# Strassen's seven products for the outputs of chunk pairs in a fused GateLoop and PReLU MLP kernel

## The chip, the cores and the metric

The kernel runs on one core of a Trainium2 chip. The metric is the device time of one execution in microseconds (us). Everything is float32.

## The reference

A gated linear attention (GateLoop) with complex gates over 768 steps, 4 batches, 8 heads of 48 dimensions, followed by an MLP of width 384, 2048, 384 over all 3072 tokens, with a PReLU whose slope is given per feature.

```python
mag = np.sqrt(a_re * a_re + a_im * a_im)
scale = np.minimum(mag, 0.999) / (mag + 1e-06)
a_re_n, a_im_n = (a_re * scale, a_im * scale)
for t in range(S):
    ar, ai = (a_re_n[:, :, t, :, None], a_im_n[:, :, t, :, None])
    new_re = ar * S_re - ai * S_im
    new_im = ar * S_im + ai * S_re
    kv = np.einsum('bhd,bhe->bhde', k[:, :, t], v[:, :, t])
    S_re, S_im = (new_re + kv, new_im)
    y[:, :, t] = np.einsum('bhd,bhde->bhe', q[:, :, t], S_re)
...
x = attn_out.transpose(0, 2, 1, 3).reshape(B * S, H * D)
h = x @ w_in
g = np.maximum(h, 0.0) + alpha * np.minimum(h, 0.0)
return g @ w_out
```

## The kernel before

The 3072 tokens are 24 chunks (units) of 128, six to a batch. Four kinds of work run side by side:

- **Gates**: nine calls of `gates`, each for one to three chunks, turn a_re and a_im into phases and products of decays with VectorE (DVE) and ScalarE (ACT), some 42 steps on a buffer of 6918 columns (`gate`, two of them), and store them in DRAM. Call g loads its inputs when call g - 2 is done.
- **Units**: `unit(u)` loads q, k, phases and decays, and goes through the chunk in levels 1, 2, 4, ... 32: DVE multiplies a 96x1024 tile in place (L634), ACT makes copies (L657, L673), TensorE (PE) forms small products (L593) that DVE or ACT mask (L617, L607). Then come transposes (L705), state sums (L717, L746, L749) and the output y of the chunk (L737, L761), which ACT copies (L775) and SyncE (SP) stores.
- **Weights**: pieces of w_in and w_out are loaded into `g_sb`, converted and put in place. This happens in the first fifth of the run.
- **MLP**: chunks are put together in groups, `sizes` = 1, 1, ten times 2, 1, 1. For a group m and each of 16 blocks f of 128 features, `features` runs three matmuls of 128x128 weights on 256 columns (128 for a single chunk) into `ps_h` (L809), of which two buffers exist; ACT takes Relu(-h) into a place of `g_sb` (L816), and DVE adds alpha - 1 times h to make the gate (L818). `outputs` then multiplies the gate of one chunk with 384 columns of w_out (L828) and sums over the 16 blocks in `ps_o`, of which there is one. At the end of a chunk ACT copies the sum (L838) into one of two rows of `top`, and SP stores it (L841). Two output matmuls follow each block of features.

`g_sb` has 36 places, in three rings, that the raw weights use first.

The order of all of this is written out. Each task is a generator that yields once before each instruction or block of them, and ORDER is a string with one letter per step; `run` walks through it. A to I are the calls of gates, J to M loads and pieces, N and O the weights, P to Z and a to m the 24 units, n the loads of the MLP's inputs, o the whole MLP. An engine runs its own instructions in this order, so an instruction that waits holds up those behind it on its engine. The rings (`R`) and times in the yields are what a planner reads; in the kernel shown here they do nothing.

Of the kernel before, what the change touches and what calls it, by code (L numbers as in the profile page):

```python
# [9 lines left out]
F32 = mybir.dt.float32  # L10
# [5 lines left out]
ALU = mybir.AluOpType  # L16
# [12 lines left out]


ORDER = (
    "ABAMBMAAAABBAAAAABAAAAAAABMAAAMNNAANBBBBBAAAKKJJJMAAAMJANAAJAAAAAAAABBOBAAONNOOBBBBBOBBBBNNOMOONBPPP"
    "LJOCKJLLCPCCCNONONPCPPPBBLLLKMMMLLKKBBJBOCPCPNNPBCCPBCBBBBBPPPPNCNBNPNNCPJJLLLLLJLLMJPCBNNPPPNBNBBBP"
    "OPPPPOCOOCPCPPOPPPPPPPMCCNOOOCOOPPDJJJMJJJDCCNNNQDPDODNPPPPDPPQNQCOPQQQQNQCPPMJJMQCOQOQNODOQQDQOJCLL"
    "LMLLLLLQDQNOOCNOORORRRnCLLLLLLLMQDRQRQRQQQQQCRRQQQQDJJKJJJMKoQoQQQoQQQLLLLLLLDONCNRNCCRNOQQOOCQCCQCC"
    "RQRCROCRQNoooooQoDQRQQDoCLooLQooQCLLLLLLRODDDRRRRRoDOoRooooooNRRRRoooRRoNDDDRoooRoRRoRoRRNRSoRSNoDRO"
    "oMJJSoooNooooooRRNSoNNoRRJJRRSSSNooooooooooSSSooooSoSSooODSSoooooSSoOoNooooJJSSnooSoSOSSLJLLLLoooRRL"
    "LLoSDSSTToJLJLLLLLLJEJToSSoSooSOSoTSToOoooTDDDDoOTooooooSSSSSSTTSSSoSToooJJKLLJLLLLoooooTSSSSSTooTTD"
    "ooooToELJJLLooooDoToooooooTDDooooooooTDTTooJLLLJoToooToooUooooooLLUoooDTTTTTooooooooooooooooooooToDD"
    "ooTooDEToooooELTJJJnTooEoTTTDTTToTDDTTTDDooooVUTTEoooooTTTLLFJoEUooUUUVUVLLLooJJoJLLLLJoooUooUoooooo"  # L40
    "ooUooooooUUUooooUUUoooooVoVoUUoooUUoVUUUEooUVEUVoUooUooUoooUoVVEEoEVKJLLLLLUUUUUUUFLLLLLJKKUUUUEVUUU"
    "UVooooooEEooooVVooVoVEEooooVoEoKVoooooooooLLLLLLLLLLVVoEVVoVEoWVoonJJEVVVVooVEEVWVooooooVVVVVVVWoEEo"
    "JLLLLEJLLLEEooooEoWVVVWVWoWEWVEVooVVLLVVoooooWWooooJooEWFooooooooooWWFFLEWEJJJKJLLLJJLLooooooWWWXooo"
    "ooWWWWoXoooooWWWWWFWooWEEFEXEEEoFoooooWWoXooWWWWWWXXoJELLLJLooXWXXXLGLJLoooWWoooXWLLLooXWWXooLXXWWXW"
    "WXoooooooLXXXXXXXXXoooooLLoooooXoXWLGJJoXXooXXXXXoYXoGXYYXooooonJLLJJLKKKLJYoXooYYYYFXXFFYoXXoooYFoo"
    "ooooooYXXFoFoKXJoYYoooGYoYoYFYXFoooooooooFGLLLJLLLLJJJJLLLoooooYYYYYooZoooooZYFFYoooooJLoooYYoFoooYY"
    "ooZGooFFFoooYooZYZZZZoooooooJFFFZYYYYYZFLLLLZLLLFYYYYYYYYYYYoooooooooaYFFFaLLLJoJLJoLLJLLKoooooooKKJ"
    "JJFZZZoooooooZZFZooooooGooZZZZZZZooZZoZooZFFFoaGGooZZooGoaZZZZZoZFZFoFFZFnLLLLLooooooooaZZZZZZZZaGGa"
    "aaZbLFLooooooaooooooaobboooHHJLooaaooooaoooooooabaaooooLJJJLLLLLJoJoooooaaaaaaaaoooaoaooaGGHGaaHoooo"
    "ooooooGbGboGGoooooooaaaaaaaabaaaaaoGboobLLJbboooGbLaaJJHHoooooLLLLLJLLJJLoLoooobcoooooobbGoobbbcbooo"  # L50
    "ooccooooobooHooooobccbbbbbbccooHbbcbooooooooocboobLLLboocGGJnJccbobbbLGGGocbbbdcccdbooooobboLLLLLLLL"
    "LLGGGGGbbbbbobLLLLooccGcoooooocJJJcoHooooococccoGococooooccooooooHoccccccGGGGGcccccccoLLJJJJKLddoGoo"
    "HoGLLLoddoddHdccoccdoooooooooooodeooddodoHdHHdoooooodeoooJJLLLLLLLJJLLJJoooooooodddHHdeoooddoHdoHHed"
    "ddoooeeeedoooIIooddooododdddHddHnddHdddoddooHeeooooddJoooooooIeeeeeoHHeooooooofoeLLdLooooeoeeeoeeeee"
    "ooooJJHJLLLLLoLLLLLLLJJJeoeoofooffoeooJoffofofffooeooooofHHHooeoeIeeeeeeHeeeeeeIgIeIoooooooffooooffo"
    "oooogHffHooHoooooofffoffffHoooeLeLLLLJJLLLLLLLLLLJJJnfJgffooooooooooofoooHgffoggffooofgIJoIHHHHHHogg"
    "gooooofffgffffggffofofgoIggfgoooooIoooooooogghhIIoooooooIogfLLLfhhoooooooIoKLLLJJhJJJJJLLLLLLLLooooh"
    "ooooIIoggoooogohhhhoghggoogoooogoioooggoogggggohggggIIIIooooooggIoggoIooooigLLLgLLLLJJLJhhhJLKoooooo"
    "ooLhhhJJoIJohooooooooooooooohhoooLLLLLihoooohihhhhoohooooiiohhooIIInIohooooooohhhhhhLiihhhhhhhhhhhoo"
    "ooooooiooIIIiioohJJLLLLLLLJJLLLLLLJoooooooIooiiooooooooooiooooiiooooooIiooooooiiIIiiiioiiIooooooojjj"  # L60
    "iooooooIooiooooooijoooijjJJjkooiLikIiooooiiiijjjjoooooiIIiiooooijLLLLLIijiiLoojjjioiLiLijLooooLoLLoo"
    "oojjjoojjjoooojjjooojjooooooojooJLjLLJoojjjjjjjjjJJJJjjjjookjjjjkooooooLookkkkkkooookooooooookkkoook"
    "noooLLLLLJJJLLJLLJJLLLLooooooLllooookkooooooooookkkkkkoooolooookkoookookooookkkoooooookkkkkkkkolllll"
    "lloooooooooooooooooollkkkLlklllJLLLLLLLLLLLoLJoooooooLooookkkkknooooolllooololoooooooooooolllllllJLJ"
    "oooooolooooollloooooooooooooooooollllooooooooolooooooooooooooooooooooooooommmoooooomommmLLLLoooooooo"
    "mmmoooLooooooooooooooooooomolllllllloooommooLlLLlmoooooooooooomnLLLLLmmoooooooooooooooooommmoooooooo"
    "oooommmmmmmooooooooomoooooooooooooooLoooooooooooooooooooooomoooooomooooomoommmmoommmmmmmoooooommmnoo"
    "oooooooooooooooooooooooooooooooooooooooooooooooooooooooooooooooooooooooooooooooooooooooooooooooooooo"
    "ooooooooooooooooooooooooooooooo")


class Ring:
# [25 lines left out]
def kernel(  # L98
# [99 lines left out]
    def step(*args, **kwargs):  # L198
# [3 lines left out]

    R = {name: Ring(n) for name, n in dict(
        KQ=3, PP=1, T=2, V=1, WQ=2, W=1, St=3, xT=2, raw0=1, raw1=1, raw2=1, g0=0, g1=0, g2=0, ot=2, top=2,
        lv=2, misc=1, y=1, h=2, o=1).items()}
    for name in (1, 4, 16, 32):
        R[name] = Ring(2 if name == 1 else 1)


    scr_of = {}  # L210
    carry = consts.tile([P, NK], F32, tag="carry")
    bias_tiny = next(column)
# [16 lines left out]
    def gates(g, b, c0, c1):  # L229
# [4 lines left out]
        TT = nc.vector.tensor_tensor  # L234
        STT = nc.vector.scalar_tensor_tensor

        flat = work.tile([P, 6 * NK * GT + 2 * NK], F32, tag="gate", name="gate", bufs=2)
        x, c, d, e = [flat[:, i * N:(i + 1) * N] for i in range(4)]
        dec = flat[:, 2 * N:4 * N].rearrange("p (m s) -> p m s", s=TL)
        wide = [flat[:, 4 * N + i * NK * (n + 1):4 * N + (i + 1) * NK * (n + 1)] for i in range(2)]  # L240
# [5 lines left out]

        for z, src in ((rows3(x), a_re), (y, a_im)):
            rows = src[b].rearrange("n i d s -> (n i d) s").rearrange("(t p) s -> p t s", p=P)
            t = yield DMA(N / 2, ("gates", g - 2))
            if last:  # L250
                nc.gpsimd.memset(z[:, :, n - 1:n], 0.0)
            nc.sync.dma_start(z[:, :, 0:n - last], rows[:, :, c0 * P + 1:c1 * P + 1 - last])
            if z is y:
                ty = t
            else:
                tx = t
# [108 lines left out]
    tops = [consts.tile([P, 2 * DM], F32, tag=f"top{i}", name=f"top{i}") for i in range(2)]  # L365
    slots = [0, 1]
    raws = {}

    g_sb = consts.tile([P, 3, 6 * MT], F32, tag="g_sb")

    def region(i):
        return (i + 2) % 3
# [181 lines left out]
    nc.gpsimd.memset(nothing, 0.0)  # L554
    nothing = nothing.bitcast(BF16)

    sizes = [1, 1] + [MC] * ((NU - 4) // MC) + [1, 1]
    group_of = [(g, c) for g, n in enumerate(sizes) for c in range(n)]

    def unit(u):  # L560
# [240 lines left out]
    def features(m, f):  # L801
# [8 lines left out]
                             start=(kk == 0), stop=(kk == NK - 1))  # L810
        if f == NF - 1:
            R["xT"].put(e)
        i, ring, half = place(m, f)
        r = yield ACT(n, e, takes=() if half == 1 else (ring,), first=True)
        gt = g_sb.rearrange("p r (f s) -> p (r f) s", f=12)[:, i:i + sizes[m]].rearrange("p f s -> p (f s)")
        nc.scalar.activation(gt, p, AF.Relu, scale=-1.0)  # L816
        r = yield DVE(n + 45, r, first=True)
        nc.vector.scalar_tensor_tensor(out=gt, in0=gt, scalar=al_1[:, f:f + 1], in1=p,  # L818
                                       op0=ALU.mult, op1=ALU.add)
        R["h"].put(r)  # L820
        return gt, r

    def outputs(m, c, f, gt, r):

        e = yield PE(0.645, r, ("w_out", f), takes=() if f else (R["o"],))
        if f == 0:
            sums[0] = ps.tile([P, DM], F32, tag="o", name="ps_o")
        nc.tensor.matmul(sums[0], lhsT=gt[:, c * P:(c + 1) * P], rhs=w_out_sb[:, f],  # L828
                         start=(f == 0), stop=(f == NF - 1))
        if c == sizes[m] - 1:  # L830
            _, ring, half = place(m, f)
            if half != 0:
                ring.put(e)
        if f == NF - 1:
            row = (sum(sizes[:m]) + c) * P
            t = yield ACT(DM, e, takes=(R["ot"],))
            ot = tops[0].rearrange("p (c e) -> p c e", c=2)[:, (row // P) % 2]
            nc.scalar.activation(ot, sums[0], AF.Copy, scale=4.0 if words else 1.0)  # L838
            R["o"].put(t)
            t = yield DMA(197, t)  # L840
            nc.sync.dma_start(out[row:row + P], ot)  # L841
            R["ot"].put(t)

    sums = {}

    def all_mlp():


        made, jobs = {}, [(m, c, f) for m, n in enumerate(sizes) for c in range(n) for f in range(NF)]
        for m in range(len(sizes)):  # L850
            for f in range(NF):
                new = yield from features(m, f)
                for _ in range(2):
                    if jobs[0][0::2] not in made:
                        break
                    j = jobs.pop(0)
                    yield from outputs(*j, *made[j[0::2]])
                    if j[2] == NF - 1:
                        break
                made[m, f] = new  # L860
        for j in jobs:
            yield from outputs(*j, *made[j[0::2]])


    for h in LEVELS[:4]:
# [55 lines left out]
```

## Time and profile before

| | |
|---|---|
| median of three runs | 814.46 us (810.97 to 818.67) |
| profiled execution | 812.23 us |
| its span, first to last instruction | 810.5 us |
| mean granted clock of PE | 0.975 |
| PE busy | 697.3 us (86%) |
| DVE busy | 564.4 us (70%) |
| ACT busy | 457.0 us (56%) |
| DMA moved | 130.58 MB, mean 161 GB/s |

Busy time is the union of an engine's instructions. Matmul records overlap, so the time that one takes from the next is read from their starts. A line such as L809 is a line of the kernel before; the rows that name a line give the operation, the tiles written and read, the size, the count, then busy time in us and mean ns, then the engine's idle time just before and what ended it. Every float32 matmul of the program leaves two matmul records and two weight loads (PEld).

The features of the MLP's groups start on PE at 104.8, 164.4, 195.4, 240.7, 303.3, 361.0, 419.3, 478.6, 537.6, 592.5, 648.7, 700.8, 746.5 and 784.0 us.

### The profile page before, as it was taken

The page shows a single profiled execution, that of the slowest core. Times are in us where ns is not written, and L with a number is a line of the kernel's source. Part 1 is how long each engine was busy: PE and PEld are TensorE (multiplying, and loading weights), DVE is VectorE, ACT ScalarE, POOL GpSimd, SP SyncE. Part 2 cuts the span into 40 slices and gives each one's busy share as a digit, 9 for nine tenths or more (in the row PEclk, how much of TensorE's full clock was granted, in tenths as well). Part 3 has the DMA queues.
Part 4 walks back from the last instruction along what each step waited for, and adds up shares of the span by engine and source line. Part 5 has one row for each costly group of instructions (what it writes and reads, how often), then busy time and mean ns, then how long its engine had stood idle before and what let it go on. Part 6 is the DMA issues. An engine that isn't in the chain of part 4 may idle for free.

```text
span 810.5 us, 26318 instructions
## 1 busy us (share of the span) xinstructions
PE 697.3 (86%) x11488; PEld 522.7 (64%) x11488; DVE 564.4 (70%) x799; ACT 457.0 (56%) x897; POOL 11.9 (1%) x49
## 2 busy tenths in 40 slices
PE   0014167899999999999999999999999999999998
PEld 0013155678777667767777777777777777777776
DVE  6889998878898778786787977887466455154122
ACT  8999894775667447746574558454644333222221
POOL 4000000000000000000000000000000000000000
PEclk9998578999999999999999999999999999999999
DMA  8989998687778596677548765784653743301010
GB/s 231 292 271 249 247 235 225 152 231 200 183 203 212 161 241 141 171 196 176 148 116 228 189 164 139 200 175 114 175 121 101 166 99 100 75 12 36 28 31 10
DMA packets 177578, 130.58 MB, mean 161 GB/s; under 512 B 66296, under 2 KB 168824, under 8 KB 177016
## 3 DMA queue, kind: packets, MB, share of 16 engines
q1 hardware_dynamic: 177464, 128.91, 60.9%
q8 instruction: 90, 1.47, 0.8%
q14 instruction: 24, 0.20, 0.1%
HBM read 100.52 MB, written 35.42 MB: 168 GB/s over the span
## 4 chain that ended last, share of the span: by engine, by line
PE 67%; ACT 14%; DVE 8%; DMA 6%; issue 3%; SPq 2%; POOL 0%; ACTq 0%; DVEq 0%; POOLq 0%
PE ps_o L828 26%; PE ps_h L809 26%; PE ps_lv L593 5%; PE ps_y L737 3%; DVE KQ L634 3%; PE ps_y L761 2%; PE ps_kv L717 2%; DMA T<-decs 2%; PE ps_kt L705 2%; ACT WQ L657 1%; DMA VL<-vsc 1%; DMA PP<-phs 1%; DMA g_sb<-in_w_in_dram 1%; ACT top L426 1%; DVE gate L304 1%
## 5 line engine op out<-in xcount | busy, mean ns | idle before, releaser
L809 PE MATMUL ps_h<-xT,w_in_sb 128*128 128x256 f32 (+1 forms) x1344 | 301.2, 355 | 0.0
L828 PE MATMUL ps_o<-w_out_sb,g_sb 128*128 128x384 f32 x768 | 296.2, 497 | 4.2 <-DVE g_sb L818 3.5
L809 PEld LDWEIGHTS ps_h<-xT,w_in_sb 128*128 128x128 f32 x1344 | 233.1, 192 | 71.3 <-DVE g_sb L818 1.8
L818 DVE SCALAR_TENSOR_TENSOR g_sb<-g_sb,al,ps_h 128x256 f32<-128x256 f32 (+1 forms) x224 | 97.6, 438 | 160.5 <-ACT g_sb L816 160.0
L816 ACT ACTIVATE g_sb<-ps_h 128x256 f32<-128x256 f32 (+1 forms) x224 | 78.4, 352 | 190.9 <-PE ps_h L809 189.9
L634 DVE TENSOR_TENSOR KQ<-KQ,T 96x1024 f32<-96x1024 f32 x120 | 145.9, 1217 | 48.4 <-PE ps_lv L593 38.0
L828 PEld LDWEIGHTS ps_o<-w_out_sb,g_sb 128*128 128x128 f32 x768 | 135.5, 190 | 53.9 <-DVE g_sb L818 6.2
L593 PE MATMUL ps_lv<-WQ 96*32 96x32 f32 x2304 | 34.4, 202 | 56.0 <-DVE WQ L576 38.8
L593 PEld LDWEIGHTS ps_lv<-WQ 96*32 96x32 f32 x2304 | 26.3, 115 | 78.1 <-DVE WQ L576 32.9
L657 ACT COPY WQ<-KQ 96x1024 f32<-96x1024 f32 x48 | 49.9, 1040 | 25.5 <-DVE KQ L634 25.5
L775 ACT COPY T<-ps_y 48x256 f32<-48x256 f32 x96 | 31.6, 364 | 39.7 <-PE ps_y L761 38.9
L737 PE MATMUL ps_y<-A,VL 64*48 64x64 f32 x2304 | 43.8, 225 | 7.3 <-issue 3.7
L607 ACT ACTIVATE A<-ps_lv,columns 128x64 f32<-128x64 f32 x144 | 37.5, 337 | 20.1 <-PE ps_lv L593 20.0
L737 PEld LDWEIGHTS ps_y<-A,VL 64*48 64x48 f32 x2304 | 40.2, 126 | 10.8 <-issue 6.5
L673 ACT COPY W<-KQ 96x512 f32<-96x512 f32 x48 | 30.6, 638 | 28.3 <-DVE KQ L634 27.2
L593 PE MATMUL ps_lv<-KQ,W 96*32 96x32 f32 x1536 | 24.2, 203 | 25.3 <-ACT W L673 24.9
L593 PEld LDWEIGHTS ps_lv<-KQ,W 96*32 96x32 f32 x1536 | 19.4, 114 | 27.8 <-ACT W L673 26.2
L705 PE MATMUL ps_kt<-ident,KQ 96*128 96x96 f32 x192 | 26.0, 260 | 13.0 <-ACT T L708 6.7
L705 PEld LDWEIGHTS ps_kt<-ident,KQ 96*128 96x128 f32 x192 | 20.9, 147 | 23.8 <-ACT T L708 9.1
L707 ACT COPY T<-ps_kt 128x384 f32<-128x384 f32 x48 | 23.1, 480 | 18.8 <-PE ps_kt L705 18.6
L717 PEld LDWEIGHTS ps_kv<-V,T 64*64 64x64 f32 x1408 | 26.6, 142 | 9.5 <-ACT T L708 5.0
L617 DVE TENSOR_TENSOR A<-ps_lv,mask 128x512 f32<-128x512 f32 x48 | 32.7, 681 | 0.0
(85 smaller groups left out, 696.5 us busy)
## 6 DMA issues: line engine op xcount, KB each, us to landing
T<-decs SPq DMA_DIRECT2D x48, 384.0 KB
PP<-phs SPq DMA_DIRECT2D x24, 387.0 KB
KQ<-in_q_dram SPq DMA_DIRECT2D x48, 192.0 KB
phs<-gate SPq DMA_DIRECT2D x14, 577.5 KB
decs<-gate SPq DMA_DIRECT2D x7, 1152.0 KB
KQ<-in_k_dram SPq DMA_DIRECT2D x40, 192.0 KB
vsc<-in_v_dram SPq DMA_DIRECT2D x24, 288.0 KB
VL<-vsc SPq DMA_DIRECT2D x48, 144.0 KB
```

The costliest lines, as they stand in the source:

```text
L593: nc.tensor.matmul(t[64 * i + j:64 * i + j + HC // 2, p], lhsT=keys(n, g), rhs=queries(n, g), start=True, stop=True)
L607: nc.scalar.activation(a[:, :, cols], t[:, :, at:at + name], AF.Copy, scale=s)
L617: nc.vector.tensor_tensor(out=a.rearrange("p l n (g t) -> p l n g t", g=2), in0=t.unsqueeze(3).to_broadcast(whole), in1=pairs[first].rearr ...
L634: nc.vector.tensor_tensor(out=x, in0=x if x0 is None else x0, in1=m, op=ALU.mult)
L657: nc.scalar.copy(z.rearrange("p i n t -> p i (n t)").rearrange("p i (m h) -> p m i h", h=h), bass.AP(tensor=KQ.tensor, offset=KQ.offset + ...
L705: nc.tensor.transpose(t[:, p], KQ[:, 1, 4 * i + p], ident[:D2, :D2])
L717: nc.tensor.matmul(kv[s][j:j + HC, n], lhsT=T[rows, n, j:j + HC], rhs=V[rows, n // 2, (n % 2) * D:(n % 2 + 1) * D], start=True, stop=True)
L737: nc.tensor.matmul(o, lhsT=Vp[h][64 * i:64 * i + 64, s, e_ * D:(e_ + 1) * D], rhs=a, start=False, stop=False)
L809: nc.tensor.matmul(p, lhsT=w_in_sb[:, f // 2, kk, f % 2 * P:(f % 2 + 1) * P], rhs=x_of[m][:, kk], start=(kk == 0), stop=(kk == NK - 1))
L816: nc.scalar.activation(gt, p, AF.Relu, scale=-1.0)
L818: nc.vector.scalar_tensor_tensor(out=gt, in0=gt, scalar=al_1[:, f:f + 1], in1=p, op0=ALU.mult, op1=ALU.add)
L828: nc.tensor.matmul(sums[0], lhsT=gt[:, c * P:(c + 1) * P], rhs=w_out_sb[:, f], start=(f == 0), stop=(f == NF - 1))
```

## The change

The last two chunks become a pair, so that `sizes` is 1, 1 and eleven times 2. Groups 0 to 2 are computed as before. From group 3 on, the outputs of a pair are a product of two by two blocks: rows are the two chunks, the inner dimension is halved (features 0 to 1023 and 1024 to 2047), and the columns are halved (192 each). Strassen's scheme in Winograd's form takes seven products of blocks, P1, P2, T2, T3, T4, T1 and P3, of eight matmuls on 192 columns each, where eight products would be 32 matmuls on 384 columns. The blocks of gates are kept by quarters (four blocks f of one chunk, 512 columns) in `spread`, 13 quarters in all. S1 to S4, sums of gate blocks, are eight DVE operations per pair on whole quarters; sums of blocks of w_out are made once (`twist`, `twist_last`). The products are read out of the two halves of one PSUM tile, P1 by ACT, the others by DVE, which adds what was summed before and writes parts of the result.

A half of a product follows each block of features; P1 and S3 come in the second half of the pair's own features, the others in those of the next pair.

`spread`, the sums of w_out, `g_sb` and the gates of call 1 share one SBUF area. Of `gate` there is one buffer left, and from call 3 on call g loads when call g - 1 is done. ORDER is new.

```diff
     R = {name: Ring(n) for name, n in dict(
...
-        lv=2, misc=1, y=1, h=2, o=1).items()}
+        lv=2, misc=1, y=1, h=2, o=1, sums=0, fourth=0).items()}
...
+    GATE = 6 * NK * GT + 2 * NK
+    QUARTER, HALF = NF // 4, DM // 2
+    shared = consts.tile([P, 18 * MT + GATE], F32, tag="shared")
+    g_sb = shared[:, 0:18 * MT].rearrange("p (r e) -> p r e", r=3)
+    spread = shared[:, 0:13 * QUARTER * P].rearrange("p (h f s) -> p h f s", f=QUARTER, s=P)
...
-        flat = work.tile([P, 6 * NK * GT + 2 * NK], F32, tag="gate", name="gate", bufs=2)
+        if g in (1,):
+            flat = shared[:, 18 * MT:18 * MT + GATE]
+        else:
+            flat = work.tile([P, GATE], F32, tag="gate", name="gate", bufs=1)
...
-            t = yield DMA(N / 2, ("gates", g - 2))
+            t = yield DMA(N / 2, ("gates", g - 2 if g < 3 else g - 1))
...
-    sizes = [1, 1] + [MC] * ((NU - 4) // MC) + [1, 1]
+    sizes = [1, 1] + [MC] * ((NU - 2) // MC)
+    FIRST = 3
...
+            r = yield ACT(n, e, takes=() if f % QUARTER else (R["fourth"],) * 2, first=True)
+            if f % QUARTER == 0:
+                two = sorted(free[0:2])
+                free[0:2] = []
+                quarter[m, f // QUARTER] = two
+            a, b_ = quarter[m, f // QUARTER]
+            gt = spread[:, a:b_ + 1:b_ - a, f % QUARTER]
+            p = p.rearrange("p (c s) -> p c s", c=2)
...
+    def twist():
+        for name, dst, x, y, op in (("T3", T3, B22, B12, ALU.subtract), ("T2", T2, T3, B11, ALU.add),
+                                    ("T4", T4, B21, T2, ALU.subtract)):
+            for i in range(2):
+                some = slice(i * F2 // 2, (i + 1) * F2 // 2)
+                t = yield DVE(F2 * HALF // 2, ("gates", 1), ("w_out", NF - 1))
+                nc.vector.tensor_tensor(out=dst[:, some], in0=x[:, some], in1=y[:, some], op=op)
...
+    def seven(m, made):
...
+        def product(blocks, w, name, after, let_go=True):
+            if not bank:
+                bank.append(ps.tile([P, 2, HALF], F32, tag="o", name="ps_o"))
+                bank.append(0)
+            z = bank[0][:, bank[1] % 2]
+            bank[1] += 1
+            for i in range(F2):
+                h = blocks[i // QUARTER]
+                e = yield PE(0.325, after[i // QUARTER], known.get(name), takes=() if i else (R["sums"],))
+                nc.tensor.matmul(z, lhsT=spread[:, h, i % QUARTER], rhs=w[:, i], start=i == 0, stop=i == F2 - 1)
...
+        z, e = yield from product(A11, B11, "P1", [F(0), F(1)], let_go=False)
+        for i in range(2):
+            t = yield DVE(QUARTER * P, F(i), takes=(R["fourth"],))
+            S3[i] = free.pop(0)
+            TT(out=whole(S3[i]), in0=whole(A11[i]), in1=whole(A21[i]), op=ALU.subtract)
...
+        t = yield ACT(HALF, e)
+        nc.scalar.activation(p1, z, AF.Copy, scale=four)
...
+        z, e = yield from product(A12, B21, "P2", [F(2), F(3)], let_go=False)
+        tx = yield DVE(HALF, e, t, takes=(R["ot"],))
+        STT(out=ot[:, 0, 0:HALF], in0=z, scalar=four, in1=p1, op0=ALU.mult, op1=ALU.add)
...
+        z, e = yield from product(A21, B12, "T1", [ready["S1", 0], ready["S1", 1]])
+        t = yield DVE(HALF, e, t)
+        STT(out=ot[:, 1, HALF:DM], in0=z, scalar=four, in1=u3, op0=ALU.mult, op1=ALU.add)
+        td = yield DMA(197, t, ty)
+        nc.sync.dma_start(out[row + P:row + 2 * P], ot[:, 1])
+        R["ot"].put(td)
+        t = yield DVE(HALF, e, t)
+        STT(out=u2, in0=z, scalar=four, in1=u2, op0=ALU.mult, op1=ALU.add)
...
+        z, e = yield from product(A12, B22, "P3", [ready["S4", 0], ready["S4", 1]])
+        t = yield DVE(HALF, e, t)
+        STT(out=ot[:, 0, HALF:DM], in0=z, scalar=four, in1=u2, op0=ALU.mult, op1=ALU.add)
...
         for m in range(len(sizes)):
+            if m == FIRST:
+                yield from twist()
+            if m >= FIRST:
+                later.append(dict(m=m, steps=seven(m, made), over=False, needs=0))
             for f in range(NF):
                 new = yield from features(m, f)
...
+                yield from some(2)
                 made[m, f] = new
```

## The prediction

> **What bounds the kernel now.** I read the page's slices first, then busy time by stretch, then TensorE (PE) in order of time, then who waits, last the groups by form.
>
> ```profile
> span 810.5 us, 26318 instructions
> PE 697.3 (86%) x11488; PEld 522.7 (64%) x11488; DVE 564.4 (70%) x799; ACT 457.0 (56%) x897; POOL 11.9 (1%) x49
> PE   0014167899999999999999999999999999999998
> DVE  6889998878898778786787977887466455154122
> ```
>
> PE is full from about the ninth slice (180 us) to the end. The chain that ended last says the same: its two largest parts are the output matmuls (L828, 26%) and the feature matmuls (L809, 26%). Before 180 us gates, loads and the first units' chains set the pace. The next view is busy time by stretch (PE, PEld, DVE, ACT, POOL):
>
> ```profile
> 240.00:300.00 60.00, 56.25 (x1039) 41.97 (x1040) 46.76 (x64) 33.31 (x67) 0.25 (x3) 1.00 0.77 204
> 300.00:360.00 60.00, 58.26 (x960) 43.03 (x959) 49.57 (x66) 40.12 (x75) 0.11 (x1) 1.00 0.66 164
> 540.00:600.00 60.00, 60.00 (x939) 45.12 (x938) 36.47 (x49) 32.91 (x68) 0.12 (x1) 1.00 0.57 144
> 700.00:811.00 111.00, 106.90 (x923) 79.06 (x921) 32.68 (x65) 25.85 (x77) 0.00 (x0) 1.00 0.10 26
> ```
>
> From 240 to 540 us PE is busy 291.8 of 300 us, at a granted clock of 1.00, and VectorE (DVE) 237.9 (79%). Later DVE has much room. So a saving on PE after 180 us comes off the end, if DVE can keep pace.
>
> **What a matmul costs.** A float32 matmul of the program leaves two records, each with a weight load. Records overlap, so starts are what counts:
>
> ```profile
> 797.28 0.81 PE L828 MATMUL ps_o<-w_out_sb,g_sb 128*128 128x384 f32 x2
> 797.93 0.83 PE L809 MATMUL ps_h<-xT,w_in_sb 128*128 128x128 f32 x6
> 798.60 0.81 PE L828 MATMUL ps_o<-w_out_sb,g_sb 128*128 128x384 f32 x2
> 653.90 1.46 PE L809 MATMUL ps_h<-xT,w_in_sb 128*128 128x256 f32 x6
> 655.19 1.45 PE L828 MATMUL ps_o<-w_out_sb,g_sb 128*128 128x384 f32 x4
> ```
>
> Two passes of 384 columns take 797.93 - 797.28 = 0.65 us, 0.323 each; six of 128 take 0.67, 0.111 each; six of 256 take 655.19 - 653.90 = 1.29, 0.215 each. A pass of 192 isn't in the trace; it lies between 0.111 and 0.215, and by the line through them at 0.163. That the 128-column passes follow at 0.111 although a weight load lasts 190 ns shows that loads overlap.
>
> **The change, part by part.**
>
> *Seven products (m from 3 on, ten pairs).* Removed per pair: 32 matmuls, 64 passes of 0.323 = 20.6 us. Added: 7 x 8 matmuls, 112 passes of 0.163 = 18.3 us. Saved 2.4 us a pair, **-24 us** in all. Bounds: with 0.161 (half of 0.323) -26; if a 192-column pass took as long as its weight load, 0.190, 21.3 us a pair, a loss of 6.4 us. I take -24, as the 128-column row refutes the second.
>
> *Last two chunks as one pair.* 192 passes of 0.111 become 96 of 0.215: 21.3 to 20.6, **-0.7**. At the very end before, PE waited 0.72 us for the last gate of a chunk and then ACT copied for 0.49; after, the last product waits for no feature and a DVE read of about 0.41 follows: **-0.8**. The last pair needs both chunks, then 20.6 us of features and six products (15.6 us). By ORDER unit 23 is finished with about 72 us of PE work left (31 before), so the store and load of its y (an issue at 777.8 for a y ended at 773.6) are covered by some 17 us of other PE work; without that cover they would cost about 5 us.
>
> *Work added to DVE.* Rows for the sizes:
>
> ```profile
> L617 DVE TENSOR_TENSOR A<-ps_lv,mask 128x512 f32<-128x512 f32 x48 | 32.7, 681 | 0.0
> L746 DVE TENSOR_TENSOR St<-St,T 96x384 f32<-96x384 f32 x44 | 24.2, 549 | 0.4
> L818 DVE SCALAR_TENSOR_TENSOR g_sb<-g_sb,al,ps_h 128x256 f32<-128x256 f32 x160 | 75.7, 476 | 105.4 <-ACT g_sb L816 105.1
> L818 DVE SCALAR_TENSOR_TENSOR g_sb<-g_sb,al,ps_h 128x128 f32<-128x128 f32 x64 | 21.9, 344 | 55.2 <-ACT g_sb L816 54.9
> ```
>
> Per pair: eight sums of 128x512, 0.68 each (0.60 from start to start in a row of them), and seven reads of 192 columns from PSUM, between 0.344 and 0.476, so 0.41 (0.33 start to start): 8.3 us at most, 7.1 net; 71 to 83 over ten pairs. Sums of w_out: eight of 768 columns at about 0.95, 7.6. Sixteen fewer L818 in the last pair, -3. DVE goes from 564 to about 640 of 800 us. ACT loses twenty copies of 0.49 and gains ten of about 0.33: -6.5 us, off the path. What hides DVE's work is PE; I counted ORDER's letters with row durations (a sum along the list, no simulation). Between the feature starts of pairs 4 and 10 PE has 323 us of work and DVE 294: 91%. The same count for before gives 339 and 246, and 345 us passed. DVE's longest surplus over PE within a group is 7.4 us before and 8.3 after. So it fits, barely: **+1** for lost slack, 0 to 10.
>
> *The hand-offs of the sums.* Before, an output sum ran for 16 matmuls and ACT read it: 24 hand-offs. After there are 4 of those and 70 products. Two products lie in the halves of one PSUM tile. If the halves are free of each other, PE is a whole product (2.6 us and a feature step) ahead: cost 0. If the next product must wait until the one before has been read, the gap is 0.16 (a pass lasts 0.486, its successor starts after 0.323) + 0.09 to the reader's start (807.00 to 807.09 at the end of the trace) + 0.41 + 0.04 = 0.70 us, mostly behind one feature block of 1.29 us. So DVE may be 0.6 us late for nothing. How late is it? The waits of DVE from 240 to 540 us, and the instructions on `ps_h` in that window:
>
> ```profile
> DVE g_sb L818 <- ACT g_sb L816: 28.2, 30, 2.6
> ```
>
> ```profile
> L818 DVE SCALAR_TENSOR_TENSOR g_sb<-g_sb,al,ps_h x81: 450/476/489, 242.5 to 537.0; 128x256 f32<-128x256 f32 x81
> ```
>
> Only 30 of 81 found DVE waiting; start of L818 less the end of its ACTIVATE is 0.77 us in the mean, over 1.3 in a quarter, and what exceeds 0.6 averages 0.47; after 660 us 0.13. By ORDER 26 hand-offs have one feature block between (19 x 0.47 + 7 x 0.13 = 10 us), 11 have up to 2.3 us (x 0.25 = 3), 5 in the last pair none (5 x 0.7 = 4), and product T1, read twice with 1.1 to 2.4 us of unit and gate work between the reads in six pairs, adds about 4: 21 us. Against that, the new order puts 0.65 us of DVE work in front of an L818 where the old put 1.05 (groups 3 to 9), so I shrink it to **+12**, with bounds 0 and 33 (lateness half again larger). I take the waiting side, since the nearest rows, the hand-offs of ps_o, all wait for the reader.
> The Trainium skill (PSUM — Partial Sum Buffer, section PSUM bank collisions raise a hardware error) speaks against the change here: two engines must not be in one bank and partition quadrant at once, whichever columns they use, so accesses are to be ordered by bank and not by address. By it the halves are one accumulator (+12 in the sum, 801); by addresses alone they are two (+0, 789). No run shown so far tells.
>
> *Quarters and twisted weights.* The gates of features go to quarters of a shared buffer. ACT waits for two free ones at every fourth f; eight of a pair and two for a difference are held, of 13, and the product that frees the next stands ahead of the waiting features in PE's own queue: 0. A write split in two runs of 128 has the size it had: 0. The sums of w_out are made once, while DVE has group 3 ahead of it; uncovered they'd cost their 7.6 us, inside the bound above.
>
> *One gate buffer from the third group on.* Loads of gates g wait for g-1 instead of g-2. In the trace group 4's loads were issued at 154.8 and 173.4, group 3's decays at 193.0: such overlap goes. Groups 7 and 8 were issued after g-1 was done or nearly (365.8 after 360.5; 460.4 after 441.6). A group serves three units, some 87 us, and was computed in 65 (187.5 to 252.7): **0**; uncovered, at the start, 5. The group's two loads stand in SP's queue, as before; POOL's memset stays.
>
> *Order and queues.* Up to the features of group 3 both orders hold the same work (PE 124 and 124 us, DVE 198 each), reached at 240.7 us: **0**, within 4. DVE's reads for P2 and T4 now wait for a free output row, a job that was ACT's; behind them stand the units' multiplications. The previous store is issued half a group (some 16 us) earlier: 0, unless SP's queue is stuck (its longest wait there is 20.5 us).
>
> **Sum.** -24 - 0.7 - 0.8 + 1 + 12 + 0 = -12.5. The profiled execution took 812.23 (span 810.5 and 1.7 around it), 2.2 under the median of 814.46: 799.7, and 802 from the median. I write **801**.
>
> **Rivals.** (1) *Free hand-offs*: halves independent, DVE in step: 812.2 - 25.5 + 1 = 788, 789 to 790 from the median. For it: distinct addresses; against it: one tile. (2) *DVE becomes the bound*: slower. In pairs 4 to 9 DVE must be filled to 91%; the trace shows 79%, with PE and ACT results late. If it stays at 79%, the 294 us take 372 where PE needs 323: +49, so 812 - 25 + 49 = 836. The gain is gone below 294 / (323 + 25) = 84%. For it: both queues run in order and meet at every product; against it: 18.4 of 20 us were reached at 20 to 40 us, and PE-bound stretches made DVE wait. (3) *Gain cancelled*: hand-offs at 20 to 33 us: 808 to 821. (4) *The products aren't cheaper*, passes at 0.190: 812 + 6 + 12 = 830; the 128-column passes speak against it.
>
> **Chances.** About 1% is what a measurement of this kernel can tell from no change: 806.3 and 822.6. Forecast (794 to 808) 0.46, of which 0.12 above 806; (1) 0.20; (2) 0.20; (3) 0.12; (4) 0.02. Faster 0.34 + 0.20 = 0.54; same 0.12 + 0.12 = 0.24; slower 0.22. The range reaches from (1) less a microsecond or so to half of (2): 787 to 826; the forecast's own is 794 to 808.
>
> **What would show it.** Right: 1120 passes of 192 columns, starting 0.163 us apart; product starts waiting on DVE for 10 to 20 us in all, most after T1 and in the last pair; DVE near 640 us busy. Wrong: no such waits (789); PE idle in 300 to 650 us well over 20 us with DVE at 80% (rival 2); passes of 0.19; PE idle before 240 us for gates.

## The result: slower by 12%

| | before | after |
|---|---|---|
| median | 813.19 us (810.97 to 818.67, four runs) | 912.13 us (906.58 to 916.18, four runs) |
| profiled execution, span | 812.23, 810.5 us | 906.58, 904.9 us |
| mean granted clock of PE | 0.975 | 0.945 |

The ratio is 1.120 (95% interval 1.112 to 1.129). These are the span, busy time and slices of the page after:

```profile
span 904.9 us, 27249 instructions
PE 716.0 (79%) x11872; PEld 603.8 (67%) x11872; DVE 639.4 (71%) x941; ACT 438.1 (48%) x863; POOL 12.0 (1%) x49
PE   0014578999999976998778879889898888898897
DVE  7898998787989865768944678776868664652422
PEclk9997679999999988999988989999999999999999
```

PE is no longer full: holes begin at the 15th slice (about 320 us), and the granted clock falls in the same places. DVE has holes there as well, so it isn't the bound. Up to group 3 nothing is lost: its features start at 240.9 us (240.7 before). Busy time by stretch (PE, PEld, DVE, ACT, POOL, then the granted clock):

```profile
240.00:300.00 60.00, 57.32 (x960) 44.56 (x953) 54.96 (x78) 34.41 (x69) 0.12 (x1) 1.00 0.67 173
300.00:360.00 60.00, 45.15 (x775) 37.98 (x767) 40.30 (x53) 25.96 (x49) 0.22 (x2) 0.91 0.45 111
540.00:600.00 60.00, 55.26 (x961) 46.85 (x963) 49.28 (x70) 32.54 (x66) 0.22 (x2) 0.97 0.58 153
```

From 300 to 360 us PE lost 13 us to before (45.15 for 58.26), and DVE was at 67%: both stood still, each for the other. All of PE's waits there, 14.8 us, are for DVE; DVE's longest, 11.2 us in all, are gates that wait for ACT's Relu of PE's features. What PE waited for from 240 us on (us in all, times, longest), one line of before first:

```profile
PE ps_o L828 <- DVE g_sb L818: 0.6, 2, 0.4
```

```profile
PE ps_o L939 <- DVE shared L840: 54.8, 28, 4.9
PE ps_o L939 <- DVE top L972: 8.0, 4, 5.0
PE ps_o L939 <- DVE top L1001: 7.8, 4, 2.7
PE ps_o L939 <- DVE top L981: 4.6, 3, 2.4
PE ps_o L939 <- DVE top L986: 3.2, 4, 1.7
```

L939 is a product's matmul. L972 to L1001 are reads of the products before it, the hand-offs of the forecast, about 25 us with L991. But the first row of after is a gate being written (L840, L818 before), and that wait is in no step of the forecast. One of these waits, from the timeline:

```profile
482.11 1.46 PE L821 MATMUL ps_h<-xT,w_in_sb 128*128 128x256 f32 x6
483.25 0.35 DVE L991 SCALAR_TENSOR_TENSOR top<-ps_o,top 128x192 f32<-128x192 f32 x1
483.61 0.38 ACT L838 ACTIVATE shared<-ps_h 128x256 f32<-128x256 f32 x1 [2.13 <-PE ps_h L821]
483.99 1.22 DVE L646 TENSOR_TENSOR KQ<-WQ,T 96x1024 f32<-96x1024 f32 x1
485.12 1.58 DVE L360 TENSOR_TENSOR gate<-gate 128x576 f32<-128x576 f32 x3
486.62 0.47 DVE L840 SCALAR_TENSOR_TENSOR shared<-shared,al,ps_h 128x256 f32<-128x256 f32 x1
487.15 2.93 PE L939 MATMUL ps_o<-w_out_sb,shared 128*128 128x192 f32 x8 [3.58 <-DVE shared L840]
```

The product at 487.15 is T1 of group 5; it reads quarters 11 and 4. The sum before it was read by 483.60 (L991). The gate at 486.62 is block 8 of group 6, and goes to quarters 2 and 12. T1 needs nothing of it. But one instruction writes both quarters, with a stride from the one to the other, and the program's waits treat everything from 2 to 12 as written by it. So the product waits for the newest gate, which stands on DVE behind a unit's multiplication and three of the gates' steps. In the program's waits 31 halves of products (four matmuls on one quarter) wait so beyond what they read. In all 31 the quarter lies between the two of such a write; where it doesn't, no half waits beyond its need.

The pause has a second price, the granted clock (the column after POOL):

```profile
482.80:486.20 3.40, 0.77 (x4) 0.34 (x2) 3.37 (x7) 1.06 (x2) 0.00 (x0) 1.00 0.36 97
486.20:493.00 6.80, 5.85 (x22) 4.84 (x24) 1.39 (x6) 0.32 (x1) 0.00 (x0) 0.50 0.44 173
```

The clock fell to 0.50 at 486.2 us, 2.6 us into the 3.58 us of idleness, and stayed there to 493.0. The eight passes took 2.73 us (487.15 to the next features at 489.88). Elsewhere they take 1.30:

```profile
277.24 1.46 PE L939 MATMUL ps_o<-w_out_sb,shared 128*128 128x192 f32 x8
278.54 1.46 PE L821 MATMUL ps_h<-xT,w_in_sb 128*128 128x256 f32 x6
```

From 240 us on the trace of after holds 14 such stretches of 3.4 or 6.8 us, the first at 329 and the last at 790 us; that of before holds none from 141 to 810 us. The Trainium skill (TensorE: Matmul & The Clock Gate, section What's actually happening) says that an idle window of about 3.4 us halves the clock and a busy one restores it; the trace agrees in kind: the clock fell after 3.4 us in which PE was busy for 0.77, and came back after 6.8 us, the second half of them busy.

**Where the 94 us of span went.** From the first feature matmul of group 3 to the last matmul, each matmul's time being taken to the start of the next (so a wait counts to what stands ahead of it), in us; the kernels named e are those below:

| | features | outputs | units | sum |
|---|---|---|---|---|
| before | 218.6 | 229.4 | 118.3 | 566.3 |
| after | 291.5 | 227.6 | 141.5 | 660.5 |
| e1_slots | 251.6 | 220.1 | 127.9 | 599.6 |
| e3_both | 230.1 | 216.8 | 128.0 | 574.9 |
| e8_unread | 218.0 | 210.3 | 127.5 | 555.8 |

With each pass at the median of its size (0.112, 0.163, 0.216 and 0.323 us) the features and outputs of before are 425.5 us and those of after 400.7: the 25 us of the forecast are there. Passes in the half-clock stretches add some 20 us to them after (none before), and gaps some 98 (22 before), 82 of it in front of products.

### The profile page after: what moved, and what is told of

Read it like the earlier page. It is cut to its first block, busy times and chain, and to the rows that moved or that the text cites. A ratio compares the mean times of both kernels' runs of the same rounds, so it can differ in the third digit from the quotient of the medians.

```text
span 904.9 us, 27249 instructions
## 1 busy us (share of the span) xinstructions
PE 716.0 (79%) x11872; PEld 603.8 (67%) x11872; DVE 639.4 (71%) x941; ACT 438.1 (48%) x863; POOL 12.0 (1%) x49
## 4 chain that ended last, share of the span: by engine, by line
PE 47%; DVE 22%; ACT 14%; DMA 5%; issue 5%; SPq 1%; ACTq 0%; DVEq 0%
PE ps_h L821 17%; PE ps_o L939 17%; DVE KQ L646 7%; PE ps_lv L605 3%; DVE shared L840 3%; PE ps_o L852 3%; PE ps_y L749 3%; DMA T<-decs 2%; PE ps_y L773 2%; ACT WQ L669 2%; PE ps_kv L729 2%; ACT shared L838 2%; ACT T L787 1%; DMA VL<-in_v_dram 1%; DMA shared<-in_w_out_dram 1%
## 5 line engine op out<-in xcount | busy, mean ns | idle before, releaser
L821 PEld LDWEIGHTS ps_h<-xT,w_in_sb 128*128 128x128 f32 x1248 | 228.4, 197 | 35.3 <-issue 0.6
L840 DVE SCALAR_TENSOR_TENSOR shared<-shared,al,ps_h 128x256 f32<-128x256 f32 (+1 forms) x208 | 94.1, 454 | 137.0 <-ACT shared L838 136.6
L838 ACT ACTIVATE shared<-ps_h 128x256 f32<-128x256 f32 (+1 forms) x208 | 76.2, 367 | 235.3 <-PE ps_h L821 207.3
L646 DVE TENSOR_TENSOR KQ<-KQ,T 96x1024 f32<-96x1024 f32 x120 | 146.1, 1218 | 45.1 <-PE ps_lv L605 34.9
L939 PE MATMUL ps_o<-w_out_sb,shared 128*128 128x192 f32 x640 | 133.8, 352 | 47.1 <-DVE shared L840 37.8
L939 PEld LDWEIGHTS ps_o<-w_out_sb,shared 128*128 128x128 f32 x640 | 111.5, 200 | 59.5 <-DVE shared L840 44.1
L939 PE MATMUL ps_o<-shared 128*128 128x192 f32 x480 | 101.0, 350 | 32.9 <-DVE shared L840 17.0
L939 PEld LDWEIGHTS ps_o<-shared 128*128 128x128 f32 x480 | 82.5, 199 | 43.3 <-DVE shared L840 19.9
L852 PE MATMUL ps_o<-w_out_sb,shared 128*128 128x384 f32 x128 | 54.1, 514 | 5.0 <-DVE shared L840 3.6
L749 PE MATMUL ps_y<-A,VL 64*48 64x64 f32 x2304 | 46.2, 233 | 4.6 <-issue 4.6
L749 PEld LDWEIGHTS ps_y<-A,VL 64*48 64x48 f32 x2304 | 43.2, 132 | 7.0 <-issue 6.5
```

The source lines that it names most:

```text
L646: nc.vector.tensor_tensor(out=x, in0=x if x0 is None else x0, in1=m, op=ALU.mult)
L749: nc.tensor.matmul(o, lhsT=Vp[h][64 * i:64 * i + 64, s, e_ * D:(e_ + 1) * D], rhs=a, start=False, stop=False)
L821: nc.tensor.matmul(p, lhsT=w_in_sb[:, f // 2, kk, f % 2 * P:(f % 2 + 1) * P], rhs=x_of[m][:, kk], start=(kk == 0), stop=(kk == NK - 1))
L939: nc.tensor.matmul(z, lhsT=spread[:, h, i % QUARTER], rhs=w[:, i], start=i == 0, stop=i == F2 - 1)
```

## The experiments

Theory A: the write into two quarters makes products wait. B: the hand-offs of the sums do. C: the order, the one gate buffer, or DVE near its limit; later expectations split C into D (DVE is full), O (the order) and G (the one gate buffer) and add H (the reader's queue stands still before each read). Times are medians; ratios are to the kernel before, run on the same chip.

**e1_slots: other quarters, written out as a list so that none in use lies between the two of a write.** No product waits beyond what it reads.

```diff
-                two = sorted(free[0:2])
-                free[0:2] = []
+                two = list(next(picks))
+                for h in two:
+                    free.remove(h)
...
-            S3[i] = free.pop(0)
+            S3[i] = next(picks)
+            free.remove(S3[i])
```

> The changed kernel with another choice of quarters: a pair of quarters is chosen so that no quarter that a product has still to read lies between the two. The same instructions, the same order, the same work. Theory A (a gate write that goes to two quarters counts, for the waits that the program sets, as if it covered all between them, so that products wait for the newest gate): the 28 waits of L939 on L840 (54.8 us of PE idle) go to almost none, with them most of the half-clock stretches after 240 us; 815 to 840 us. Theory B (the hand-offs of sums alone cost the time): under 1% of change, 900 to 912. Theory C (new order, one gate buffer, DVE at its limit): DVE is late whichever wait shows it, the waits move to other instructions, 885 to 912.

842.27 us, ratio 1.035 (1.027 to 1.042): 70 us less (60 between the two profiled executions), with not one instruction of the work changed, and 2 us above the band of A. The waits of products for gates are gone; the hand-offs lead the list:

```profile
PE ps_o L946 <- DVE top L1009: 10.6, 7, 2.7
PE ps_o L946 <- DVE top L980: 7.8, 5, 4.2
PE ps_o L946 <- DVE top L989: 5.3, 4, 2.4
```

**e11_near: the nearest free pair of quarters.** 8 of the 31 waits are left.

```diff
-                two = sorted(free[0:2])
-                free[0:2] = []
+                pairs_ = [(sum(h not in free for h in range(a + 1, b)), b - a, a, b)
+                          for a in free for b in free if a < b]
+                two = list(min(pairs_)[2:])
+                for h in two:
+                    free.remove(h)
```

> The changed kernel with another choice of the two quarters of a write: the nearest free pair, in place of the two that came free first. Of the 31 products that wait for a gate which they do not read 8 are left (e1_slots: none). Theory A (each such wait costs): 912 - 23/31 of 70 = 860, 850 to 870. If it is not the waits but something else that e1_slots changed: near 912 or near 842.

859.75 us, ratio 1.058 (1.055 to 1.061), where 860 was expected: 31, 8 and 0 such waits give 912, 860 and 842. The trace counts the same eight:

```profile
PE ps_o L942 <- DVE shared L843: 15.2, 8, 3.5
```

Theory A is shown, with its dose.

**e2_actread and e3_both: ScalarE takes each sum out of PSUM, DVE adds from SBUF.** e2 is that alone, e3 with e1's quarters.

```diff
+        def read(z):
+            zs = tops[1][:, 3 * HALF:4 * HALF]
+            nc.scalar.activation(zs, z, AF.Copy, scale=four)
+            return zs
...
-        STT(out=u3, in0=z, scalar=four, in1=u2, op0=ALU.mult, op1=ALU.add)
+        TT(out=u3, in0=read(z), in1=u2, op=ALU.add)
```

> The changed kernel with the quarters as they were, but ScalarE copies each product's sum out of PSUM into SBUF (seven reads a pair, six of them new) and DVE adds from there. A product then waits for ScalarE's copy, not for DVE. Theory A: the waits on L840 stay, 5 to 20 us less than the changed kernel: 892 to 907. Theory B: the 25 us of PE waits on L972, L981, L986, L991 and L1001, and the half clock behind them, go: 860 to 885. Theory C: no change, 905 to 915.

> Both edits together: quarters with nothing live between them, and sums read by ScalarE. Theory A with B as its smaller part: 790 to 810, the saving of PE work of 25 us then shows in part. Theory C: 870 or more.

899.82 us (ratio 1.105, 1.099 to 1.111) and 824.33 us (1.016, 1.009 to 1.022). e2 won 12 us, as A had it, and e3 another 18 on e1: hand-offs cost, but A is the larger part. e3 stayed 14 us above its band; in it PE still waits 13.3 us for the copies.

**e8_unread: what all hand-offs cost.** The kernel of e3, its copies taking columns of w_out in place of the sums.

```diff
-            nc.scalar.activation(zs, z, AF.Copy, scale=four)
+            nc.scalar.activation(zs, B11[:, 0], AF.Copy, scale=four)
```

> The kernel of e3_both in which ScalarE's copies take 192 columns of w_out in place of the product's sum: it leaves out the reading of the products, so no product waits for a reader, and no copy for a product; all instructions and their sizes stay. Theory B (hand-offs): the 13.3 us of waits on the copies go and the half-speed passes behind them, 800 to 812. Theory D or O: 816 to 826, the waits turn up at the next instruction of TensorE.

803.16 us, ratio 0.986 (0.981 to 0.991): 21 less than e3, 39 less than e1 (from which it also differs in the reader). This is what the products are worth when nobody reads them. The longest waits are now in the units:

```profile
PE ps_lv L605 <- ACT W L685: 6.5, 9, 1.3
PE ps_kt L717 <- ACT T L720: 4.9, 3, 2.6
```

**e9_twobanks and e10_twobanks_dve: products by turns in two tiles.** Where no unit uses the tile of `ps_kt`, a product goes there; 53 of 69 successions are then between different tiles. e9 starts from e3, e10 from e1 (DVE reads).

```diff
-            z = bank[0][:, bank[1] % 2]
+            if next(banks) == "m":
+                z = ps.tile([P, HP, D2], F32, tag="misc", name="ps_m").rearrange("p n d -> p (n d)")[:, 0:HALF]
+            else:
+                z = ps.tile([P, 2, HALF], F32, tag="o", name="ps_o")[:, 0]
```

> The kernel of e3_both with the products in two tiles that do not share a bank, where the order leaves one free: 53 of the 69 pairs of successive products then lie in ps_o and in the tile of ps_kt by turns (in the stretches in which no unit uses it), 16 stay behind each other in ps_o. Nothing is left out. e8_unread without any hand-off took 803, e3_both with 69 of them 824. Theory B (hand-offs through one bank): 53/69 of the 21 us come back, 806 to 813, and the wait of ps_o for the copy falls from 13.3 to under 5 us. Theory O (what is left is the order; e8_unread gained by not making ScalarE wait for the products): 818 to 826.

> As e9_twobanks, but VectorE reads the products itself, as in the change (the kernel of e1_slots, 842, with two tiles). Theory B: of the 39 us between e1_slots and e8_unread 53/69 come back, 808 to 820, near e9_twobanks, as the reader's lateness no longer matters where the tiles alternate. Theory D (VectorE's queue is what is late, whoever waits): 825 to 842.

818.44 us (ratio 1.006, 1.003 to 1.008) and 828.38 (1.019, 1.017 to 1.021). In e9 PE's wait for the copies fell from 13.3 to 2.7 us as expected, but the time only by 6: it lies in the band of O, not of B. e10 won 14 on e1 and lies in the band of D (a late DVE queue). So, as far as these two runs tell, PE's own wait is the smaller part of what reading costs. ScalarE still stood 49 us before copies, as its queue reached them ahead of the products' ends:

```profile
ACT top L938 <- PE ps_o L950: 30.7, 22, 4.2
ACT top L938 <- PE ps_m L950: 18.4, 12, 2.3
```

**e12_deferred and e13_deferred_dve: the read behind the first half of the next product**, where the two lie in different tiles (41 of 69).

```diff
+        def later_if_free(tail):
+            if banks[turn_of[0] - 1:turn_of[0] + 1] in ("om", "mo"):
+                pending.append(tail)
+            else:
+                yield from tail
...
                 if i == QUARTER - 1:
+                    while pending:
+                        yield from pending.pop(0)
                     yield 0
```

> The kernel of e9_twobanks, with the copy of a product and its addition put behind the first half of the next product wherever the two lie in different tiles (41 of the 69 successions; 28 stay in one tile with the copy at once). ScalarE then meets the copy when the product has long ended. In e9_twobanks ScalarE stood 49 us before a copy (30.7 on ps_o and 18.4 on ps_m), with the gates and the units' weights behind it; in e8_unread it stood for none. Theory H (the part of e8_unread's gain that e9_twobanks did not bring comes from ScalarE no longer standing before copies): those 49 us fall to about 20, and the time to 805 to 813. Theory O (the rest is the order): 816 to 822.

> As e12_deferred, with VectorE reading the products itself (the kernel of e10_twobanks_dve, 828, with the reads put behind the first half of the next product in 41 of 69 successions). Theory H says the same of VectorE's queue: it meets a read when the product has ended, and TensorE does not wait for the read: 812 to 820. If VectorE's lateness is what counts wherever the read stands: 825 to 835, since 28 successions remain in one tile, 12 more than before.

816.46 us (ratio 1.003, 1.000 to 1.007) and 836.4 (1.028, 1.021 to 1.035). ScalarE's waits before copies fell from 49 to 35 us only, and the gain of 2 on e9 is within what can be told: the band of H (805 to 813) is missed. With DVE as the reader it became slower than e10 and lies above both bands. 28 successions share a tile where 16 did, and a unit's transposes, which use the second tile, waited 6.5 us for late reads (1.1 in e10); which of the two it was isn't shown. So how the other 15 us of e8 divide between the readers' queues and the order stays open. e12 is the best whole version found: level with the kernel before, not ahead of it.

**e5_nosums and e6_pool: the eight sums of a pair, nearly left out, or on GpSimd** (both from e3).

```diff
-            return spread[:, h]
+            return spread[:, h, :, 0:2]
```

```diff
-            TT(out=whole(S3[i]), in0=whole(A11[i]), in1=whole(A21[i]), op=ALU.subtract)
+            nc.gpsimd.tensor_tensor(out=whole(S3[i]), in0=whole(A11[i]), in1=whole(A21[i]), op=ALU.subtract)
```

> The kernel of e3_both (quarters chosen so that no live one lies between the two of a write, products read out by ScalarE), with each of the eight sums of a pair cut from 128x512 to 128x8 elements: it leaves out nearly all of the additions that the seven products need, and keeps their places, their waits and everything else. VectorE loses 80 times about 0.6 us, 48 us of the 436 that it is busy between 240 and 820 us in e3_both. Theory D (what is left of the loss comes from VectorE, full to 90% from 240 to 420 us, so that every result of a unit and every gate is late): 790 to 806. Theory O (the order with one gate buffer starves TensorE whatever the outputs cost, as in e4_classic): 815 to 826, group starts within 5 us of e3_both's. Theory B (the hand-offs of the sums, 13.3 us of waits in e3_both and the slow clock behind them): 812 to 822, since the copies by ScalarE still stand behind the same gates.

> The kernel of e3_both with the eight sums of a pair on GpSimd, which is idle, in place of VectorE: nothing is left out. Theory D: 795 to 812, near e5_nosums, if GpSimd has a sum of 128x512 done in under 2 us; if it takes longer, the products S2, S4 wait for it and the time goes above 824, with TensorE's waits naming GpSimd. Theory O: 815 to 830. It also tells what 80 sums cost on GpSimd, which no run so far shows.

817.01 us (ratio 1.003, 1.000 to 1.006) and 841.83 (1.034, 1.030 to 1.038). Taking 39 us off DVE's busy time (637.2 to 598.4) gives 7, so DVE's fullness (theory D) is a small part. GpSimd makes it worse, by some 17 us on e3:

```profile
L981 POOL TENSOR_TENSOR shared<-shared 128x512 f32<-128x512 f32 x20 | 30.5, 1544 | 0.0
```

Such a sum takes 1.48 to 1.64 us there in the mean of its four lines (0.68 on DVE). That is under the 2 us of the expectation, yet the time is far above its band. PE waited only 1.0 us for GpSimd itself. But DVE's own work on SBUF slowed: 80 sums of 0.68 us less would leave it 583 us, and it was busy 627.0. L646 rose from 1217 to 1293 ns in the mean, the gates' products L360 from 338 to 420. Their medians hardly moved (1216 to 1220 and 236 to 234 ns); the longest rose from 1.22 to 2.33 and from 0.76 to 1.82 us. So a few instructions were held up and the others ran as before.

**e4_classic and e7_classic_two: the new order with outputs as before**, one gate buffer and two. The letters o were moved so that each output step stands where a product's did. e4 leaves out the last 18 of the 384 output matmuls and the stores of the last two chunks; e7 does them all, but some of its values come out wrong, so it stands for its time alone.

```diff
-    FIRST = 3
+    FIRST = 13
...
-        if g in (1,):
+        if g % 2:
...
-            t = yield DMA(N / 2, ("gates", g - 2 if g < 3 else g - 1))
+            t = yield DMA(N / 2, ("gates", g - 2))
```

(The last two edits are e7's.)

> The changed kernel without the seven products: all thirteen groups are computed with 384-column output matmuls into g_sb, as groups 0 to 2 are. Order of all other tasks, one gate buffer and the last pair as in the changed kernel; the output steps follow each block of features at the places that the products had. It isolates order and gate buffer. Theory A or B: 805 to 825, as before the change. Theory C: 850 or more.

> The kernel of e4_classic (new order, all outputs as before in 384 columns), with all 768 output matmuls done (e4_classic leaves out the last 18, 11.6 us) and with two gate buffers in turn, loads of gates g waiting for g-2 as in the kernel before. Theory G (the wait for the one gate buffer makes the units late): group starts 15 to 40 us earlier than in e4_classic from group 4 on, 815 to 840 in all. Theory O (the order itself: where it puts the units, the loads and the gates): group starts within 6 us of e4_classic's, 855 to 867 in all.

851.49 us (ratio 1.046, 1.040 to 1.052) and 868.35 (1.066, 1.059 to 1.073). e4 lies in the band of C. Two gate buffers bring nothing: e7's features start 3 to 7 us later than e4's all along. That the pair is slow doesn't convict the order: already group 3 starts at 256 to 259 us, where after and before have 241, so moving the letters itself did harm. The order's share can't be read from these two.

## Why the prediction was wrong

Forecast 801 us, in a range of 787 to 826; measured 912.

- *Seven products, -24, and the last pair's features, -0.7*: right. Eight passes of 192 columns take 1.30 us, 0.1625 each (0.163 forecast), and the passes of features and outputs came out 24.8 us shorter.
- *Work added to DVE*: right in amount, 639.4 us of about 640. Its cost, +1 with bounds 0 and 10, was nearer 7, if what e5 saves on e3 is the measure.
- *Quarters and twisted weights, 0*: **the step that failed**, 70 us (e1). "the product that frees the next stands ahead" held, and so did "A write split in two runs of 128 has the size it had". What was priced was the size of the write and the room for it; what was not asked is what the write is taken to cover, and who then waits for it. Each of the 31 waits is a chain PE, ACT, DVE in the middle of a stretch that PE should fill, so it also takes in whatever stands in DVE's queue ahead of the gate.
- *The clock*: no step priced it. Some 20 us of the loss in features and outputs are passes at half clock around pauses; e1 has some 7 of them left, so 13 of the 61 us that its row of the table is shorter are the clock.
- *Hand-offs, +12 with bounds 0 and 33*: right in kind. Two halves of one tile are one accumulator, as was chosen and as the Trainium skill (PSUM — Partial Sum Buffer, section PSUM bank collisions raise a hardware error) has it: the reads of the product just before lead e1's list of waits. The size was wrong: 25 us of waits after, and e8 less e1 is 39 us. The lateness of DVE was taken from the trace of before, in which DVE read no output sum. In the new program DVE itself stands 41 us before products from 240 us on (30 in e1), a term that the sum left out. That this standing is what makes the difference is argued, not shown: e12 and e13 did not bear it out.
- *One gate buffer, 0*: nothing speaks against it; e7 gained nothing from two, though in an order that had been harmed.
- *Order, 0 within 4*: right up to group 3 (240.9 for 240.7). Later the units' matmuls take 9 us more than before in e1, e3 and e8 alike (127.5 to 128.0 for 118.3). By how much the order and by how much DVE's sums make that wasn't separated.
- *Rivals*: rival 2 had the sign but not the cause. DVE's share fell to 67% in 300 to 360 us as PE did, instead of bounding it at 79%, and taking sums off DVE won 7 us. The two-sided wait that it described ("both queues run in order and meet at every product") is the right picture; the meeting that cost most was one that nothing in the arithmetic asked for.

In numbers of the table: after to e1 -60.9, e1 to e3 -24.7, e3 to e8 -19.1; e8 is then 10.5 below before, where the arithmetic alone gives 25. What holds the other 14 us isn't known; 9 of them stand in the units' column.

## What to carry to other kernels

When one instruction writes two places far apart, ask what its dependence covers, not only what it writes: here every place between the two counted as written, and choosing places with none in use between them won 70 us without touching the work. A saving of 25 us on a full engine is soon spent if it multiplies the places at which that engine must wait for a reader; count the hand-offs and take the reader's queue as part of the price. A wait of a few us on TensorE can also slow what follows: in the case shown, 3.58 us of waiting made the next product and feature block, 2.6 us of work, take 5.4 (487.15 to 492.57).

## What the hardware showed that was not expected

The granted clock fell to 0.50 at pauses of a few us in the middle of a busy stretch, for 3.4 or 6.8 us at a time, and eight passes of such a stretch took 2.73 us for 1.30. One fall came after a stretch of 3.4 us in which PE was still busy for 0.77. GpSimd took 1.48 to 1.64 us for a sum that DVE does in 0.68, and in that run two of DVE's operations between SBUF tiles were 6% (L646) and 24% (L360) longer in the mean, because a few of them took about twice as long.
